# First loads of a layer kernel: block 0 of x and weight piece 0 in two 64-row halves on both queues, blocks 2 and 3 of x in one load

## The chip, the cores and the metric

One core of one Trainium2 chip runs the kernel. The metric is device microseconds of one execution, the median of several runs. PE (TensorE) does the matrix multiplications and transposes, DVE (VectorE) and ACT (ScalarE) the elementwise work, POOL (GpSimd) some DMA, and SP (SyncE) issues most loads. ACT issues a few loads too, from its own instruction stream: while it issues one it does nothing else.

## The reference

A pre-norm transformer layer in bf16, sequence length S = 2048, width D = 512:

```python
h  = x + A(layernorm(x))      # A: qkv = n @ wqkv; 32 heads of 16; each position attends to
                              # 8 positions pos, pos-2, ..., pos-14 (masked below 0); @ wo
h2 = h + B(layernorm(h))      # B: (relu(n @ W_gate) * (n @ W_up)) @ W_down, F = 1376
# layernorm(x) = (x - mean) / sqrt(var + 1e-5) over the 512 columns of a row
```

## The kernel before, in words

The 2048 rows of x are 16 blocks of 128 rows; a chunk is 4 blocks, and the kernel goes through 4 chunks, with the work of neighbouring chunks interleaved. A table of ranks (`RANK`) fixes the order of all steps on every engine; the change does not touch it. Ahead of the planned steps stands `setup()`, which issues the first loads and builds small constants.

**The first loads.** `x_sm` holds all of x; `x_sm[:, j, :]` is block j, 128 rows of 1 KB. `wqk_sb[:, j, :]` is weight piece j: rows 128j to 128j+127 of the q and k columns, 128 rows of 2 KB. SP issued, in this order: block 0, block 2, piece 2, block 4, block 5, piece 3; and behind them blocks 6 and 7 (L343), the v weights (L344), chunks 2 and 3 of x (L346), the output weights (L348). ACT issued block 1, block 3, piece 0, piece 1, and behind these four its activation table is loaded (L328). Loads of x are L325 and of pieces L327 in the profile.

**Semaphores of the loads.** The framework gives the loads of SP and ACT eight semaphores in turn. A ninth load waits until the first, whose semaphore it takes over, has landed, and so on. In the listings below these semaphores are `DMAHW0` to `DMAHW7`; an instruction that reads a loaded tile waits for the semaphore of its load.

**Layer norm of chunk 0.** For blocks 0, 2 and 3 DVE takes the statistics (L492) and aggregates them (L495); for block 1 ACT sums the row (L476) and its squares (L482). ACT makes the scale factor of each block out of these with a logarithm and an exponential (L505 or L508, then L512). DVE writes the normalized rows (L553, L551 for block 1; tile `row`). PE transposes them (L582, tile `bank`), ACT evicts the transposes of blocks 0 and 1 (L598) and DVE those of blocks 2 and 3 (L596) into a tile `quad`. DVE's order is: statistics 0, 2, 3, with the aggregations between, then rows 0, 1, 2, 3. ACT's order is: sum 1, logarithm 0, squares 1, exponential 0, logarithms 1 and 2, exponentials 1 and 2, logarithm and exponential 3, evictions of 0 and 1.

**Projection of chunk 0.** The first six q and k tiles (L623, weights `wqk_sb`) are summed over the four pieces in the order 0 (for columns 0 to 255, blocks 0 and 1), 0 (columns 256 to 511, blocks 2 and 3), 2, 1, 3. Before all this PE multiplies zeros (L437, `warm`). The rest of the kernel, attention, output projection and the gated MLP (L1010, L1064), is not touched.

The program's first lines that matter:

```python
x_rows = A_x.rearrange("b (tb p) d -> p (b tb) d", p=P)      # P = 128, BPC = 4 blocks a chunk
w3_r = A_wqkv.rearrange("(dt p) f -> p dt f", p=P)
WQ = ([("a", 0, 2 * P, 0), ("b", 2 * P, CS, 0), ("c", 0, CS, 2), ("d", 0, CS, 1), ("e", 0, CS, 3)],)
XS = ((0, 1),)                                               # chunk 0, block 1: sums on ACT
```

Of the kernel before, what the change touches and what calls it, by code (L numbers as in the profile page):

```python
# [8 lines left out]
P = 128  # L9
# [192 lines left out]
def kernel(  # L202
# [11 lines left out]
    nc = tc.nc  # L214
    Bsz, S, D = A_x.shape
# [23 lines left out]
    BPC = CS // P  # L239
# [4 lines left out]
    x_rows = A_x.rearrange("b (tb p) d -> p (b tb) d", p=P)  # L244
# [20 lines left out]
    x_sm = sb.tile([P, NTB, D], BF16, name="x_sm")  # L265
    wqk_sb = sb.tile([P, NT, 2 * D], BF16, name="wqk_sb")
# [39 lines left out]
    def f_load(n, i):  # L306
        if n == "d":
            lo, hi = (0, 5) if i == 0 else (5, NFF)
            nc.sync.dma_start(
                wd_sb[:, lo:hi, :], B_W_down[lo * P:hi * P, :].rearrange("(ft p) n -> p ft n", p=P))  # L310
            if FTAIL and i:
                nc.sync.dma_start(wd_sb[:FTAIL, NFF, :], B_W_down[NFF * P:F, :])
        elif n == "g":
            nc.sync.dma_start(wgu_sb[:, :, 0, :], B_W_gate.rearrange("(dt p) f -> p dt f", p=P))
        else:
            w = B_W_up.rearrange("(dt p) f -> p dt f", p=P)
            nc.sync.dma_start(wgu_sb[:, 2 * i:2 * i + 2, 1, :], w[:, 2 * i:2 * i + 2, :])

    def setup():

        w3_r = A_wqkv.rearrange("(dt p) f -> p dt f", p=P)
        for q, n, j in ((nc.sync, "x", 0), (nc.scalar, "x", 1), (nc.sync, "x", 2), (nc.scalar, "x", 3), (nc.sync, "w", 2),
                        (nc.scalar, "w", 0), (nc.sync, "x", BPC), (nc.scalar, "w", 1), (nc.sync, "x", BPC + 1), (nc.sync, "w", 3)):
            if n == "x":
                q.dma_start(x_sm[:, j:j + 1, :], x_rows[:, j:j + 1, :])  # L325
            else:
                q.dma_start(wqk_sb[:, j:j + 1, :], w3_r[:, j:j + 1, 0:2 * D])  # L327
        nc.scalar.preload_act_table_set("natural_log_exp_and_others")  # L328
        V.memset(warm[:], 0.0)
        make_identity(nc, identity[:])  # L330
        nc.gpsimd.memset(eps_t[:, 0:1], EPS)
        nc.gpsimd.memset(eps_t[:, 1:2], EPS * D * D)
        nc.gpsimd.iota(ci[:], pattern=[[0, 1]], base=0, channel_multiplier=1)
        nc.gpsimd.iota(sel_i[:], pattern=[[1, H]], base=0, channel_multiplier=0)
        nc.gpsimd.iota(sp_i[:], pattern=[[1, H], [0, DQ]], base=0, channel_multiplier=0)
        nc.gpsimd.iota(sm_i, pattern=[[0, 4], [1, H]], base=0, channel_multiplier=0)
        nc.gpsimd.iota(mk_i[:], pattern=[[1, PADL]], base=0, channel_multiplier=0)
        nc.gpsimd.memset(kT[:, :, 0:PADL], 0.0)
        nc.gpsimd.memset(vT[:, :, 0:PADL], 0.0)


        for j in range(BPC + 2, 2 * BPC):
            nc.sync.dma_start(x_sm[:, j:j + 1, :], x_rows[:, j:j + 1, :])  # L343
        nc.sync.dma_start(wv_sb[:], w3_r[:, :, 2 * D:3 * D])  # L344
        for tk in range(2, NCK):
            nc.sync.dma_start(x_sm[:, tk * BPC:(tk + 1) * BPC, :], x_rows[:, tk * BPC:(tk + 1) * BPC, :])  # L346

        nc.sync.dma_start(wo_sb[:], A_wo.rearrange("(p t) f -> p t f", t=NT))  # L348
        if "g" not in LATE:
            f_load("g", 0)  # L350

        for n, (op, by) in enumerate(((ALU.arith_shift_right, 2), (ALU.bitwise_and, H - 1),
                                      (ALU.arith_shift_right, 5))):
            V.tensor_scalar(out=tmp[:, n:n + 1], in0=ci[:], scalar1=by, scalar2=None, op0=op)
        V.tensor_copy(out=cf[:, 0:3], in_=tmp[:])
        V.tensor_scalar(out=cf[:, 2:3], in0=cf[:, 2:3], scalar1=1.0 * DIL, scalar2=None, op0=ALU.mult)
        V.tensor_scalar(out=cf[:, 3:4], in0=cf[:, 2:3], scalar1=4.0 * DIL, scalar2=None, op0=ALU.add)
        V.tensor_scalar(out=sel[:], in0=sel_i[:], scalar1=cf[:, 0:1], scalar2=None, op0=ALU.is_equal)
        V.tensor_scalar(out=spread[:], in0=sp_i[:], scalar1=cf[:, 1:2], scalar2=None, op0=ALU.is_equal)
        V.tensor_scalar(out=same[:], in0=sm_i, scalar1=cf[:, 1:2], scalar2=None, op0=ALU.is_equal)  # L360
        for hf in range(2):
            V.tensor_scalar(out=mask[:, hf, :], in0=mk_i[:], scalar1=cf[:, 2 + hf:3 + hf],
                            scalar2=None, op0=ALU.is_ge)
# [242 lines left out]
    for tk in range(NCK):  # L606
# [353 lines left out]
        for f0 in range(0, NFT, 2):  # L960
# [77 lines left out]
            n, fs = len(fts), P if fts[-1] < NFF else FTAIL  # L1038
# [66 lines left out]
    for o in plan.ops:  # L1105
        n = o.key[0] if o.key else ""
# [7 lines left out]
    with tc.manual_schedule():  # L1114
        setup()
        for op in todo:
            if op.fn is not None:
                op.fn()
# [35 lines left out]
```

## Time and profile before

| | |
|---|---|
| timed runs | 191.07, 191.41, 191.52 us (median 191.41) |
| the profiled execution | 190.84 us, of which the span from the first to the last instruction is 189.0 us |
| granted TensorE clock | 1.000 |
| PE busy | 183.6 us (97%) |
| DVE, ACT, POOL busy | 149.3, 116.9, 25.1 us |
| chain that ended last | PE 94%, ACT 3% |

Times in a row are microseconds from the span's start unless marked ns. A row of the timeline gives the start, the length, the engine (an added q means its sequencer, so the issue of a DMA), the line, what was written and read, and in brackets the idle time of the engine before it and what ended it. A row of the DMA issues gives how many of a kind were issued, KB each, and the time from issue to landing. Queue q1 holds the loads of SP, q10 those of ACT.

### The profile page before, as it was taken

What the parts mean: (1) busy time and instruction counts of PE and PEld (TensorE: products, weight loads), DVE (VectorE), ACT (ScalarE), POOL (GpSimd) and SP (SyncE); (2) the same over time, 40 slices, a digit from 0 to 9 for tenths busy, and PEclk for the clock granted to TensorE, in tenths of its full rate; (3) what the DMA queues carried; (4) which work ended last, traced back from release to release, by engine and by line L of the source; (5) the groups of instructions that cost most, each with busy time, mean ns of one, the idle gap of its engine ahead of it and who ended that gap; (6) DMA issues with size and microseconds to landing.
All of it is one profiled execution on the core that took longest, in us unless ns stands there. A gap on an engine that the chain in (4) does not pass through costs nothing.

```text
span 189.0 us, 2973 instructions
## 1 busy us (share of the span) xinstructions
PE 183.6 (97%) x1077; PEld 92.3 (49%) x1077; DVE 149.3 (79%) x226; ACT 116.9 (62%) x241; POOL 25.1 (13%) x46
## 2 busy tenths in 40 slices
PE   7798999999999999999999999999999999999994
PEld 7554455654454445544444464444445445454543
DVE  6999999999999999999999986999758401315233
ACT  4689999965676868923656686134874602675700
POOL 3000503300000032310051250025100000000000
DMA  5998488980987979993238998659923500102014
GB/s 156 330 343 351 92 200 141 194 166 0 184 229 185 292 153 182 183 214 63 59 68 153 173 179 238 114 111 180 214 49 88 107 4 0 55 3 56 0 62 132
DMA packets 27742, 26.96 MB, mean 143 GB/s; under 512 B 14704, under 2 KB 23248, under 8 KB 27728
## 3 DMA queue, kind: packets, MB, share of 16 engines
q1 hardware_dynamic: 23696, 15.47, 30.4%
q0 software_dynamic: 3312, 10.49, 29.3%
q10 hardware_dynamic: 720, 0.82, 1.3%
q8 instruction: 8, 0.13, 0.3%
q14 instruction: 6, 0.05, 0.1%
HBM read 8.42 MB, written 2.10 MB: 56 GB/s over the span
## 4 chain that ended last, share of the span: by engine, by line
PE 94%; ACT 3%; ACTq 1%; issue 0%; DVE 0%
PE bank L1010 37%; PE bank L623 22%; PE bank L1064 20%; PE bank L933 7%; PE bank L973 3%; PE bank L680 3%; PE bank L582 1%; PE bank L732 1%; ACT L328 1%; ACT quad L598 1%; ACTq L327 0%; ACTq L325 0%; PE bank L777 0%; ACT row L548 0%; ACT junk L482 0%; ACT rs L508 0%
## 5 line engine op out<-in xcount | busy, mean ns | idle before, releaser
L1010 PE MATMUL bank<-quad,wgu_sb 128*128 128x512 bf16 x320 | 72.4, 379 | 0.0
L1010 PEld LDWEIGHTS <-wgu_sb 128*128 128x128 bf16 x320 | 31.0, 98 | 37.1 <-issue 1.3
L1064 PE MATMUL bank<-wd_sb,gT 128*128 128x512 bf16 (+3 forms) x198 | 39.6, 355 | 0.0
L1020 ACT ACTIVATE gr<-bank 128x512 bf16<-128x512 f32 x40 | 23.1, 604 | 13.1 <-PE bank L1010 10.2
L623 PE MATMUL bank<-quad,wqk_sb 128*128 128x512 bf16 (+1 forms) x134 | 30.0, 370 | 0.0
L1064 PEld LDWEIGHTS <-gT 128*128 128x128 bf16 (+1 forms) x198 | 18.5, 98 | 19.9
L1017 ACT CAST up_sb<-bank 128x512 bf16<-128x512 f32 x30 | 16.9, 602 | 14.9 <-PE bank L1010 12.3
L674 DVE TENSOR_TENSOR big<-quad,kT 128x4096 bf16<-128x4096 bf16 x11 | 25.1, 2286 | 0.0
L852 DVE TENSOR_TENSOR big<-big,vT 128x4096 bf16<-128x4096 bf16 x11 | 24.7, 2289 | 0.0
L1041 DVE TENSOR_TENSOR gT<-gr,up_sb 128x1024 bf16<-128x1024 bf16 x20 | 13.6, 689 | 9.4 <-ACT gr L1020 6.3
L895 POOL DMA_DIRECT2D big<-big x14 | 12.4, 883 | 64.5 <-DVE big L852 55.0
L623 PEld LDWEIGHTS <-wqk_sb 128*128 128x128 bf16 x134 | 14.9, 113 | 12.2 <-issue 0.6
L1072 DVE SCALAR_TENSOR_TENSOR row<-bank,iv,x_sm 128x512 bf16<-128x512 f32 (+2 forms) x10 | 6.2, 642 | 18.4 <-PE bank L1064 18.2
L482 ACT ACTIVATE junk<-x_sm,sm 128x512 bf16<-128x512 bf16 x17 | 12.2, 720 | 9.6 <-DVE x_sm L944 9.5
L623 PE MATMUL bank<-quad,wv_sb 128*128 128x512 bf16 x64 | 16.2, 380 | 0.0
L933 PE MATMUL bank<-wo_sb,quad 128*128 128x512 bf16 x64 | 14.8, 379 | 0.0
L855 DVE TENSOR_TENSOR big<-big 128x1024 bf16<-128x1024 bf16 (+2 forms) x20 | 12.9, 662 | 1.8 <-DMA big<-big 1.7
L944 DVE SCALAR_TENSOR_TENSOR x_sm<-x_sm,bank 128x512 bf16<-128x512 bf16 x16 | 10.7, 679 | 2.7 <-PE bank L933 2.7
L631 ACT CAST kT<-bank 128x512 bf16<-128x512 f32 x16 | 9.2, 591 | 3.2 <-PE bank L623 3.2
L631 ACT CAST quad<-bank 128x512 bf16<-128x512 f32 x16 | 9.2, 586 | 3.2 <-PE bank L623 3.2
L623 PEld LDWEIGHTS <-wv_sb 128*128 128x128 bf16 x64 | 6.9, 114 | 7.1 <-issue 1.3
L820 POOL DMA_DIRECT2D big<-ex x12 | 6.8, 591 | 23.8 <-DVE st L492 18.3
(85 smaller groups left out, 178.5 us busy)
## 6 DMA issues: line engine op xcount, KB each, us to landing
big<-big POOLq DMA_DIRECT2D x14, 512.0 KB, 5.4
big<-ex SPq DMA_DIRECT2D x20, 128.0 KB, 3.7
big<-ex POOLq DMA_DIRECT2D x12, 128.0 KB, 4.0
wgu_sb<-in_B_W_gate_dram SPq DMA_DIRECT2D x1, 1376.0 KB, 9.6
wgu_sb<-in_B_W_up_dram SPq DMA_DIRECT2D x2, 688.0 KB, 5.1
wd_sb<-in_B_W_down_dram SPq DMA_DIRECT2D x2, 640.0 KB, 5.4
x_sm<-in_A_x_dram SPq DMA_DIRECT2D x2, 512.0 KB, 7.4
x_sm<-up_sb POOLq DMA_DIRECT2D x4, 256.0 KB, 3.4
```

Source lines behind the costliest of these rows:

```text
L623: nc.tensor.matmul(mm.t[:, lo:hi], lhsT=wv_sb[:, dt, t:D:NT] if c == 2 else wqk_sb[:, dt, c * D + t:(c + 1) * D:NT], rhs=xnT.t[:, dt, lo:h ...
L631: nc.scalar.copy(out=o, in_=mm.t[:])
L674: V.tensor_tensor(out=pb.t[:].rearrange("p (t w) s -> p t w s", t=2), in0=q4, in1=k4, op=ALU.mult)
L852: V.tensor_tensor(out=mt.t[:], in0=ab.t[:], in1=v8, op=ALU.mult)
L855: V.tensor_tensor(out=mt.t[:, 0:n, :], in0=mt.t[:, 0:n, :], in1=mt.t[:, n:2 * n, :], op=ALU.add)
L895: nc.gpsimd.dma_start(mt.t[:, 0:4, :], mt.t[:, 4:8, :], accum_op=ALU.add)
L933: nc.tensor.matmul(od.t[:], lhsT=OT.t[:, t, j * P:(j + 1) * P], rhs=wo_sb[:, t, :], start=(t == 0), stop=(t == NT - 1 and tk not in RPE))
L1010: nc.tensor.matmul(mm.t[:fs, lo:hi], lhsT=wgu_sb[:, dt, g, ft * P: ft * P + fs], rhs=hnT.t[:, dt, lo:hi], start=(dt == 0), stop=(dt == NT ...
L1017: nc.scalar.copy(out=ub.t[:fs, i, :], in_=um.t[:fs, :])
L1020: nc.scalar.activation(out=gr.t[:fs, i, :], in_=gm.t[:fs, :], func=ACT.Relu, scale=-1.0 if tk in HX else 1.0)
L1041: V.tensor_tensor(out=gt.t[:fs, 0:n, :], in0=gr.t[:fs, 0:n, :], in1=ub.t[:fs, 0:n, :], op=ALU.mult)
L1064: nc.tensor.matmul(od.t[:, c0:c1], lhsT=gts[ft].t[:fs, ft % 2, j * P:(j + 1) * P], rhs=wd_sb[:fs, ft, c0:c1], start=(ft == 0), stop=(ft == ...
```

## The change

Block 0 of x is fetched as rows 0 to 63 by SP and rows 64 to 127 by ACT; weight piece 0 likewise, as the third load of each queue. Block 1 goes to SP's second place; ACT's second load is now blocks 2 and 3 together, 128 rows of 2 x 1 KB. Piece 2 is SP's fourth load and piece 1 ACT's fourth. Behind them nothing changes in order. SP has one load more than before, ACT as many.

```diff
     def setup():
 
         w3_r = A_wqkv.rearrange("(dt p) f -> p dt f", p=P)
-        for q, n, j in ((nc.sync, "x", 0), (nc.scalar, "x", 1), (nc.sync, "x", 2), (nc.scalar, "x", 3), (nc.sync, "w", 2),
-                        (nc.scalar, "w", 0), (nc.sync, "x", BPC), (nc.scalar, "w", 1), (nc.sync, "x", BPC + 1), (nc.sync, "w", 3)):
+        hp = P // 2
+        hp = P // 2
+        for q, n, j in ((nc.sync, "x", 0), (nc.scalar, "x", 0), (nc.sync, "x1", 1), (nc.scalar, "xx", 2), (nc.sync, "w", 0),
+                        (nc.scalar, "w", 0), (nc.sync, "w1", 2), (nc.scalar, "w1", 1), (nc.sync, "x1", BPC), (nc.sync, "x1", BPC + 1), (nc.sync, "w1", 3)):
+            lo, hi = (0, hp) if q is nc.sync else (hp, P)
             if n == "x":
+                q.dma_start(x_sm[lo:hi, j:j + 1, :], x_rows[lo:hi, j:j + 1, :])
+            elif n == "xx":
+                q.dma_start(x_sm[:, j:j + 2, :], x_rows[:, j:j + 2, :])
+            elif n == "x1":
                 q.dma_start(x_sm[:, j:j + 1, :], x_rows[:, j:j + 1, :])
+            elif n == "w":
+                q.dma_start(wqk_sb[lo:hi, j:j + 1, :], w3_r[lo:hi, j:j + 1, 0:2 * D])
             else:
                 q.dma_start(wqk_sb[:, j:j + 1, :], w3_r[:, j:j + 1, 0:2 * D])
```

On SP, the start of its program before (loads of x and of weight pieces, with the semaphores that their issue waits for; the first three wait for none):

```order
L325 DMA x_sm<-in_A_x_dram 128x512 x2
L327 DMA wqk_sb<-in_A_wqkv_dram 128x1024
L325 DMA x_sm<-in_A_x_dram 128x512
L325 DMA x_sm<-in_A_x_dram 128x512 [waits DMAHW0_49]
L327 DMA wqk_sb<-in_A_wqkv_dram 128x1024 [waits DMAHW1_49]
L343 DMA x_sm<-in_A_x_dram 128x512 [waits DMAHW2_49]
```

and now:

```order
L328 DMA x_sm<-in_A_x_dram 64x512
L332 DMA x_sm<-in_A_x_dram 128x512
L334 DMA wqk_sb<-in_A_wqkv_dram 64x1024
L336 DMA wqk_sb<-in_A_wqkv_dram 128x1024
L332 DMA x_sm<-in_A_x_dram 128x512 [waits DMAHW0_49]
L332 DMA x_sm<-in_A_x_dram 128x512 [waits DMAHW1_49]
L336 DMA wqk_sb<-in_A_wqkv_dram 128x1024 [waits DMAHW2_49]
L352 DMA x_sm<-in_A_x_dram 128x512 [waits DMAHW3_49]
```

Piece 3 (the last 128x1024) waited for the second semaphore, block 0's; it now waits for the third, that of the double block. Block 4 waited for no load and now waits for a half of block 0.

On ACT, the start of its program before, down to the sum of block 1 and the first logarithm:

```order
L325 DMA x_sm<-in_A_x_dram 128x512 x2
L327 DMA wqk_sb<-in_A_wqkv_dram 128x1024 x2
L328 ACT_TABLE_LOAD
L476 ACTIVATE junk,sm_121<-x_sm 128x512 [waits DMAHW0_49]
L508 ACTIVATE rs_131<-mv_117,eps_t 128x1 [waits DVE_49,Pool_49]
```

and now:

```order
L328 DMA x_sm<-in_A_x_dram 64x512
L330 DMA x_sm<-in_A_x_dram 128x2x512
L334 DMA wqk_sb<-in_A_wqkv_dram 64x1024
L336 DMA wqk_sb<-in_A_wqkv_dram 128x1024
L337 ACT_TABLE_LOAD
L485 ACTIVATE junk,sm_121<-x_sm 128x512 [waits DMAHW3_49]
L517 ACTIVATE rs_131<-mv_117,eps_t 128x1 [waits DVE_49,Pool_49]
```

Four loads stand ahead of the table load as before; the sum of block 1 now waits for a load of SP, not for ACT's own first one.

On DVE, the statistics of blocks 0, 2 and 3 of chunk 0 and the first normalized row, before:

```order
L492 BN_STATS st_113<-x_sm 128x6 [waits DMAHW1_49]
L495 BN_AGGR mv_117<-st_113 128x2 [waits DVE_49]
L492 BN_STATS st_114<-x_sm 128x6 [waits DMAHW3_49]
L495 BN_AGGR mv_117<-st_114 128x2 [waits DVE_49]
L492 BN_STATS st_115<-x_sm 128x6 [waits DMAHW2_49]
L553 TENSOR_SCALAR row_104<-x_sm,mv_117,rs_131 128x512 [waits Activation_49]
```

and now:

```order
L501 BN_STATS st_113<-x_sm 128x6 [waits DMAHW1_49,DMAHW0_49]
L504 BN_AGGR mv_117<-st_113 128x2 [waits DVE_49]
L501 BN_STATS st_114<-x_sm 128x6 [waits DMAHW2_49]
L504 BN_AGGR mv_117<-st_114 128x2 [waits DVE_49]
L501 BN_STATS st_115<-x_sm 128x6
L562 TENSOR_SCALAR row_104<-x_sm,mv_117,rs_131 128x512 [waits Activation_49]
```

The order of the work is the same; block 0's statistics wait for two halves, block 2's for the double block, and block 3's for no load of their own.

## The prediction

> **What bounds the kernel now.** I read the page first, then the waits of PE over the whole span, then the chain that ended last and the engines one by one over the first 8 us, and last the DMA queues in short windows. The page's first row and PE's waits:
>
> ```profile
> PE 183.6 (97%) x1077; PEld 92.3 (49%) x1077; DVE 149.3 (79%) x226; ACT 116.9 (62%) x241; POOL 25.1 (13%) x46
> ...
> PE bank L437 <- DVE warm L329: 1.0, 1, 1.0
> PE bank L582 <- DVE row L553: 1.0, 1, 1.0
> PE bank L582 <- ACT row L548: 0.5, 1, 0.5
> ```
>
> PE is busy for 183.6 of 189.0 us, and its only listed waits are three, all before 18 us. So after the start there is next to nothing in which a late start could be made up: what the first projection matmul (L623) loses or gains, the end loses or gains. The change touches only the first loads; the question is what they do to that matmul. The chain of waits at the start, times in us from the span's start, then length:
>
> ```profile
> 2.63 1.28 ACT L328
> ...
> 3.93 0.33 ACT junk L476
> ...
> 6.73 0.97 ACT quad L598 x2
> ...
> 7.74 1.28 PE bank L623 x8
> ```
>
> ACT issues its four loads, loads its table until 3.91, sums block 1 (L476) at 3.93 and goes on without a real break to the transposes' evictions (L598), which release L623 at 7.74. No load stands in this chain. DVE is as tight beside it:
>
> ```profile
> 3.30 0.69 DVE L492 BATCH_NORM_STATS2 st<-x_sm 128x6 f32<-128x512 bf16 x1
> 4.03 0.18 DVE L495 BATCH_NORM_AGGREGATE mv<-st 128x2 f32<-128x6 f32 x1
> 4.13 0.66 DVE L492 BATCH_NORM_STATS2 st<-x_sm 128x6 f32<-128x512 bf16 x1
> 4.83 0.18 DVE L495 BATCH_NORM_AGGREGATE mv<-st 128x2 f32<-128x6 f32 x1
> 4.95 0.70 DVE L492 BATCH_NORM_STATS2 st<-x_sm 128x6 f32<-128x512 bf16 x1
> 5.67 0.41 DVE L553 TENSOR_SCALAR row<-x_sm,mv,rs 128x512 bf16<-128x512 bf16 x1
> ...
> 5.45 0.18 ACT L512 ACTIVATE rs<-rs 128x1 f32<-128x1 f32 x1
> ```
>
> The statistics of blocks 0, 2 and 3 (3.30, 4.13, 4.95) run one behind the other up to the first normalized row at 5.67, and ACT's factor for that row (L512) is done at 5.63: two chains that meet within 0.04 us. From 5.67 to 7.74 there are 2.07 us of transposes and evictions that the change leaves alone.
>
> **The change part by part.** What the loads did before (landing counted from the issue). The first pair was issued at 0.74 on both queues, the second, as half of each "x2" row, at about 1.17 (ACT) and 1.20 (SP):
>
> ```profile
> x_sm<-in_A_x_dram ACTq DMA_DIRECT2D x1, 128.0 KB, 2.7
> x_sm<-in_A_x_dram SPq DMA_DIRECT2D x1, 128.0 KB, 2.5
> ...
> x_sm<-in_A_x_dram ACTq DMA_DIRECT2D x1, 128.0 KB, 3.8
> x_sm<-in_A_x_dram SPq DMA_DIRECT2D x1, 128.0 KB, 2.7
> ...
> 0.73 0.90 ACTq L325 DMA_DIRECT2D x_sm<-in_A_x_dram  x2
> 1.67 0.94 ACTq L327 DMA_DIRECT2D wqk_sb<-in_A_wqkv_dram  x2
> ...
> 0.74 0.87 SPq L325 DMA_DIRECT2D x_sm<-in_A_x_dram  x2
> 1.66 0.42 SPq L327 DMA_DIRECT2D wqk_sb<-in_A_wqkv_dram  x1
> ```
>
> So block 0 landed at 3.3, block 1 at 3.4 to 3.5, block 2 at 1.20 + 2.7 = 3.9 and block 3 at 1.17 + 3.8 = 4.97 by the rounded row (its reader started at 4.95). Block 2 had 0.2 us to spare against 4.13, block 3 none, and it needed none.
>
> *Block 0 in halves.* It may land sooner than 3.3; its reader is the first L492. But DVE's next step waits for block 2, and ACT's chain starts from the table load. Price: zero either way, up to a landing 0.2 us later.
>
> *ACT's issues.* Four before, four after. Four took 2.63 - 0.73 = 1.90 us, up to the table load. A half may take less: the shortest issue in the trace is 0.33 us (the row of 4.95 below), against 0.45 for each of ACT's two (0.90 x2), so two halves save at most 0.24. The double block may take more: the nearest row is a load of 4 blocks, 1.07 for two, so 0.54 and at most 0.09 more. The table load moves by -0.24 to +0.09 and the factor of L512 is ready at 5.39 to 5.72. I take 0, and DVE covers all of it, as follows.
>
> ```profile
> 4.95 0.33 SPq L343 DMA_DIRECT2D x_sm<-in_A_x_dram  x1
> 7.35 1.07 SPq L346 DMA_DIRECT2D x_sm<-in_A_x_dram  x2
> ```
>
> *Blocks 2 and 3 in one load.* This is the term that counts. One semaphore now stands for both, so the statistics of block 2 wait until block 3 is in as well. No row shows a load of this kind at this place. It cannot be before block 2's own 3.9, where it costs nothing. The nearest row above is block 3's 4.95, the same last byte of the same 512 KB of x. The queue counts tell which is nearer (packets, MB, share of 16 engines; q10 is ACT's queue, q1 SP's; first 3.4 to 3.8 us, then 4.6 to 5.0):
>
> ```profile
> q1 hardware_dynamic: 23, 0.03, 79.8%
> q10 hardware_dynamic: 68, 0.06, 44.3%
> ...
> q1 hardware_dynamic: 35, 0.07, 45.9%
> q10 hardware_dynamic: 35, 0.07, 45.2%
> ...
> q1 hardware_dynamic: 302, 0.29, 29.6%
> q10 hardware_dynamic: 284, 0.27, 22.6%
> ```
>
> The last two rows are 0 to 3.8 us. Two blocks are 256 rows of 1 KB and, if every engine closes each load with one small packet, 32 more: 288. ACT's queue had started 284 packets by 3.8, so all but a few of block 3 were through by then and a late rest made it 4.95. With a landing some 0.5 after the last packet (an estimate: block 2 landed at 3.9, when SP's queue had long turned to weights), an undisturbed pair would land near 4.3; with a late rest at 4.95. I take 4.4, in the middle of 3.9 and 4.95. Then L492 of block 2 starts at 4.42 instead of 4.13, +0.29, everything behind it on DVE is back to back, the first row starts at 5.96 instead of 5.67 (ACT's factor at 5.72 at the latest is hidden), and L623 starts at 8.03: **+0.3**. Bounds of the term: 0 and 4.97 - 4.13 = 0.84; more is rival B.
>
> *Weight piece 0 in halves.* The pieces on ACT's queue were issued at 1.67 and about 2.15 (the two take 0.94), the first piece on SP's (piece 2) at 1.66, and they landed after:
>
> ```profile
> wqk_sb<-in_A_wqkv_dram SPq DMA_DIRECT2D x1, 256.0 KB, 5.0
> wqk_sb<-in_A_wqkv_dram ACTq DMA_DIRECT2D x1, 256.0 KB, 5.2
> ...
> wqk_sb<-in_A_wqkv_dram ACTq DMA_DIRECT2D x1, 256.0 KB, 5.7
> ```
>
> Piece 0 landed at 6.9 and is first used at 7.74: 0.8 us to spare. The halves stand at the same depth in the queues; sooner brings nothing, and even at the 7.85 of the last ACT piece they would be in time for 8.03. Price zero.
>
> *SP's queue waits.* SP has one load more, so each later load waits for a different earlier one: block 4, which waited for none, now for a half of block 0, and piece 3 for the double block (issue at 3.87 before, about 4.4 now). Piece 3 has no spare time, as the weight loads of PE show:
>
> ```profile
> 3.87 0.44 SPq L327 DMA_DIRECT2D wqk_sb<-in_A_wqkv_dram  x1
> ...
> wqk_sb<-in_A_wqkv_dram SPq DMA_DIRECT2D x1, 256.0 KB, 5.1
> x_sm<-in_A_x_dram SPq DMA_DIRECT2D x1, 128.0 KB, 4.3
> ...
> 8.97 0.44 PEld L623 LDWEIGHTS <-wqk_sb 128*128 128x128 bf16 x3 [0.20 <-DMA wqk_sb<-in_A_wqkv_dram]
> ```
>
> It was issued at 3.87 and landed 5.1 later, at 8.97, and PE's loader took it at that moment. The load behind it was issued 1.07 us later (4.95) and landed only 0.3 later (9.25): the queue ahead sets these landings, not the issue, and the bytes ahead are the same. So I take zero. If the issue did set it, piece 3 would land at 4.42 + 5.1 = 9.5, against a need that has moved to 8.97 + 0.3 = 9.27: 0.25 more at worst. Block 4 feeds statistics of the next chunk, which no PE wait names. The loads behind (v weights, rest of x, wo, gate) may move by half a microsecond; the three waits of PE above name none of them.
>
> **Sum.** 190.84 (the profiled execution: 189.0 of span and 1.84 around it) + 0.3 = 191.1. The timed runs have their median at 191.41, 0.57 above that execution; the same +0.3 on it gives **191.7**. The forecast's own range is 191.4 to 191.98: a shift that a measurement can hardly tell from none (0.3% is 0.57 us, about what one can tell here).
>
> **Rivals.**
>
> *B, the double block shares turns with the weights: slower.* SP's queue holds half of block 0 and block 1, 192 rows, before its weight half; ACT's holds 64 + 256 = 320 rows before its own. If the engines take from the two queues in equal turns, as the 35 and 35 packets of 4.6 to 5.0 show, 128 rows of x are left on ACT's queue when SP's turns to weights. Each then lets a weight row pass, 0.459 x 6.4 / 35 = 0.084 us of one engine, and the first ones 0.798 x 6.4 / 23 = 0.22 (6.4 is 16 engines for 0.4 us). 128 x 0.084 / 16 = 0.67, plus 23 x 0.14 / 16 = 0.2 for the slow first rows: the pair lands at 4.4 + 0.87 = 5.3, L623 shifts by 1.2, and the time is 191.41 + 1.2 = **192.6** (192.0 to 193.0). It decides from a landing at 4.7 on, where the shift passes 0.57. Against it stands that ACT's queue passed 68 packets from 3.4 to 3.8 while SP's, already at weights, passed 23: block 3 went ahead of them. Also, the Trainium skill ("DMA: Bandwidth & Descriptors", the section on queues, rings and completion order) says that an engine drains a whole packet, typically 9 to 17 descriptors, from one queue before it turns to the other; by that rule the double block, some 16 rows per engine, would go ahead whole and B would fall away, which leaves the +0.3. The equal 35 and 35 neither bear this out nor refute it. Chance 0.36.
>
> *C, the halves bring a gain.* The timed runs lie 0.2 to 0.7 above the profiled one. If that is block 0 or 1 coming late in them, an earlier block 0 and a shorter ACT issue take it away: about 191.41 - 0.57 = **190.8**. For it: the two chains before 5.67 leave 0.04 us of slack. Against it: block 1, which ACT needs first, moves from first to second place, and block 2 must come by 4.13. The Trainium skill ("DMA: Bandwidth & Descriptors", the rules for kernel authors) advises against splitting a load into two partition halves, since both go over the same 16 engines; by it block 0 would land no sooner than 3.3 and C would have nothing. In this trace two loads of 128 KB issued together landed 0.2 apart, at 2.5 and 2.7, which fits. Chance 0.07.
>
> *D, nothing moves.* The double block lands by 4.13, ACT's chain stays the last: **191.4**. For it: block 2's 3.9. Against it: the last x bytes had not all started by 3.8. Chance 0.07.
>
> **How the numbers follow.** The forecast has 0.50, B 0.36, C 0.07, D 0.07. Faster by over 0.3% (below 190.84) is C, 0.07. Slower by over 0.3% (above 191.98) is B, 0.36. Within is the forecast and D: 0.57. The range 191.2 to 192.7 holds the forecast, D and some two thirds of B, and leaves out C and B's upper end, about 2 in 10.
>
> **What would show it.** Right: in the changed profile the second L492-type statistic (now L501) starts at 4.2 to 4.6, waiting for a load, the first row about 1.5 us later, and the first projection matmul at 7.9 to 8.3; the table load and ACT's sum of block 1 stand within 0.2 us of their old places; PE's wait before the transposes grows from 1.0 to about 1.3. B: that statistic starts after 4.7, with weight packets on SP's queue before the double block is in. C or D: the first projection matmul at 7.74 or before. Wrong altogether: a new PE wait for weights behind 8 us, or a shift at the start that is not found again at the end.

## The result and the profile after

| | before | after |
|---|---|---|
| timed runs, median (range), us | 191.41 (191.07 to 191.59) | 194.01 (192.24 to 195.33) |
| ratio to before, 95% interval | | 1.0113 (1.0064 to 1.0161) |
| profiled execution; its span, us | 190.84; 189.0 | 192.24; 190.5 |
| granted TensorE clock of the profiled execution | 1.000 | 0.999 |
| first projection matmul starts, us | 7.74 | 8.73 |

The change makes the kernel slower, by 1.1%; the forecast of 191.7 and its range up to 192.7 were too low. Disturbed runs (here the one of 195.33, later the one of 198.08 and the three of 196.1 to 196.85 without warm-up) are left out of all ratios and means.

The profiled execution of after is its fastest run. In it the loss lies at the start and stays: the first projection matmul comes 0.99 later and the last store is issued 1.00 later; the rest of the span's growth of 1.5 comes after that store. The last store, before and after:

```profile
186.66 0.35 ACTq L1078 DMA_DIRECT2D out_dram<-row  x1
...
187.66 0.35 ACTq L1087 DMA_DIRECT2D out_dram<-row  x1
```

The page's first row, as shown of before:

```profile
PE 183.4 (96%) x1059; PEld 93.0 (49%) x1077; DVE 149.4 (78%) x226; ACT 116.8 (61%) x241; POOL 25.1 (13%) x46
```

and PE's waits:

```profile
PE bank L591 <- DVE row L562: 1.1, 1, 1.1
PE bank L446 <- DVE warm L338: 1.0, 1, 1.0
PE bank L591 <- ACT row L557: 0.5, 1, 0.5
```

PE's work is the same (18 matmuls fewer are recorded, but as many weight loads), and its wait before the transposes has grown by only 0.1: the same 77 warm-up matmuls ended at 6.06 in this execution and at 5.16 in that of before, so part of the delay doesn't show as a wait. The chain of waits at the start names what is new (start, length, in us):

```profile
0.74 0.61 SPq L328
...
1.41 3.48 DMA x_sm<-in_A_x_dram
...
4.92 0.02 ACT junk L485
...
7.72 0.97 ACT quad L607 x2
...
8.73 0.74 PE bank L632 x5
```

Before, this chain began with ACT's issues and its table load, and no load stood in it. Now a load does: SP's second one, block 1, issued at 1.41 and landed 3.48 later, at 4.89. ACT's sum of block 1 (L485, L476 before) starts at 4.92 instead of 3.93. The two issuing engines and ACT's first work, from the timeline:

```profile
0.74 0.56 ACTq L328 DMA_DIRECT2D x_sm<-in_A_x_dram  x1
1.34 0.60 ACTq L330 DMA_DIRECT2D x_sm<-in_A_x_dram  x1
1.97 0.50 ACTq L334 DMA_DIRECT2D wqk_sb<-in_A_wqkv_dram  x1
2.50 0.60 ACTq L336 DMA_DIRECT2D wqk_sb<-in_A_wqkv_dram  x1
3.13 1.28 ACT L337 ACT_TABLE_LOAD   x1 [3.13 <-issue]
4.92 0.63 ACT L485 ACTIVATE junk<-x_sm 128x512 bf16<-128x512 bf16 x1 [0.50 <-DMA x_sm<-in_A_x_dram]
...
0.74 0.61 SPq L328 DMA_DIRECT2D x_sm<-in_A_x_dram  x1
1.41 0.81 SPq L332 DMA_DIRECT2D x_sm<-in_A_x_dram  x1
```

Every issue in these rows is longer than before. The halves take 0.56 and 0.61, though they move half the bytes of a block that took 0.45 on ACT; the load behind a half takes 0.60 on ACT and 0.81 on SP. So the table load starts at 3.13 instead of 2.63 (+0.50), ends at 4.41, and ACT then still waits 0.50 for block 1: together the 0.99. The landing alone sets this start: with the table load at its old place ACT would have waited until 4.92 just the same. DVE and PE follow:

```profile
4.38 0.69 DVE L501 BATCH_NORM_STATS2 st<-x_sm 128x6 f32<-128x512 bf16 x1 [0.16 <-DMA x_sm<-in_A_x_dram]
...
6.66 0.41 DVE L562 TENSOR_SCALAR row<-x_sm,mv,rs 128x512 bf16<-128x512 bf16 x1 [0.78 <-ACT rs L521]
7.12 1.55 PE L591 MATMUL bank<-identity,row 128*128 128x128 bf16 x16 [1.06 <-DVE row L562]
8.73 6.68 PE L632 MATMUL bank<-quad,wqk_sb 128*128 128x256 bf16 x35
```

The double block let the statistics of block 2 start at 4.38, 0.25 later than before. That delay is then covered: DVE waits 0.78 for ACT's factor before it writes the first row at 6.66. ACT's chain is the late one.

The profile explains 1.0 to 1.4 us; the ratio stands for 2.2. The granted clock of the timed runs shows where the rest may be. The run of 192.24 has 0.999, those of 193.51, 194.01 and 194.52 have 0.991. 0.9% of 192 us is 1.7 us, what one stretch of 3.4 us at half clock would take away; profiles further down show such stretches.

### The profile page after: what moved, and what is told of

Same layout as the page of the kernel before. It is cut to its first block, busy times and chain, and to the rows that moved or that the text cites. A ratio compares the mean times of both kernels' runs of the same rounds, so it can differ in the third digit from the quotient of the medians.

```text
span 190.5 us, 2958 instructions
## 1 busy us (share of the span) xinstructions
PE 183.4 (96%) x1059; PEld 93.0 (49%) x1077; DVE 149.4 (78%) x226; ACT 116.8 (61%) x241; POOL 25.1 (13%) x46
## 4 chain that ended last, share of the span: by engine, by line
PE 92%; ACT 2%; DMA 2%; issue 1%; SPq 0%; DVE 0%
PE bank L1019 36%; PE bank L632 21%; PE bank L1073 20%; PE bank L942 7%; PE bank L982 3%; PE bank L689 3%; DMA x_sm<-in_A_x_dram 2%; PE bank L591 1%; PE bank L741 1%; PE bank L786 1%; ACT quad L607 1%; ACT row L557 0%; ACT junk L491 0%; SPq L328 0%; ACT rs L517 0%
## 5 line engine op out<-in xcount | busy, mean ns | idle before, releaser
L632 PE MATMUL bank<-quad,wv_sb 128*128 128x512 bf16 x61 | 15.7, 380 | 0.3 <-issue 0.2
```

Of the source, the lines that this page charges most:

```text
L632: nc.tensor.matmul(mm.t[:, lo:hi], lhsT=wv_sb[:, dt, t:D:NT] if c == 2 else wqk_sb[:, dt, c * D + t:(c + 1) * D:NT], rhs=xnT.t[:, dt, lo:h ...
```

## The experiments

Theory 1, formed from the profile after: block 1 sits in SP's second place behind ACT's double block, which is issued 0.07 earlier and goes first. Theory 2: the cut into 64 rows itself is slow to issue and delays the load behind it. The rival for the runs at clock 0.991: they are an accident of the chip, not of PE's wait. Each time stands against the runs of before on the same chip (medians 191.58, 191.61 and 191.45 in the three groups). Of long lines the diffs show only the items that change.

**Block 1 on ACT, the double block on SP.** Everything else as after.

```diff
-                        (nc.sync, "x1", 1), (nc.scalar, "xx", 2),
+                        (nc.sync, "xx", 2), (nc.scalar, "x1", 1),
```

> The changed kernel with the second loads of the two queues exchanged: block 1 on ACT, the double block on SP. Theory 1 (rows are handed to the engines load by load in the order of issue, so in the changed kernel block 1 stood behind all of the double block, which ACT had issued 0.07 us earlier, and landed at 4.89): block 1 now lands by 4.0 and ACT's sum of block 1 waits only for the table load, at about 4.4 instead of 4.92; the first projection matmul at 8.2 to 8.4 instead of 8.73. Rival (block 1 is late because SP's queue is served worse, or because halves slow all loads): block 1 lands no sooner than 4.6 on ACT as well, and the first projection matmul stays at 8.6 or later.

Measured: 192.84 (191.88 to 194.19), ratio 1.0071 (1.0042 to 1.01). The timeline of this kernel:

```profile
1.41 0.79 SPq L329 DMA_DIRECT2D x_sm<-in_A_x_dram  x1
...
3.11 1.28 ACT L336 ACT_TABLE_LOAD   x1 [3.11 <-issue]
...
4.41 0.63 ACT L484 ACTIVATE junk<-x_sm 128x512 bf16<-128x512 bf16 x1
5.46 0.69 DVE L500 BATCH_NORM_STATS2 st<-x_sm 128x6 f32<-128x512 bf16 x1 [1.25 <-DMA x_sm<-in_A_x_dram]
```

Block 1 is now in time (ACT starts at 4.41, as its table load ends), but the double block on SP lands 4.03 after its issue instead of 3.0 on ACT, and DVE waits 1.25 for it; the first projection matmul starts at 8.92, not at the 8.2 to 8.4 that theory 1 expected. SP's second load is late whichever it is. Six runs at clock 0.999 or more average 192.45, four at 0.991 average 193.75: 1.3 us lie between.

**Only block 0 in row halves.** No double block, piece 0 whole; SP issues its half, block 1, block 3, piece 2, ACT its half, block 2, pieces 0 and 1.

```diff
-  (nc.sync, "x1", 1), (nc.scalar, "xx", 2), (nc.sync, "w", 0), (nc.scalar, "w", 0),
+  (nc.sync, "x1", 1), (nc.scalar, "x1", 2), (nc.sync, "x1", 3), (nc.scalar, "w1", 0),
```

> Block 0 in halves, but no double block and piece 0 whole: SP issues half 0, block 1, block 3, piece 2; ACT half 0, block 2, piece 0, piece 1. Theory 2 (a half load takes longer to issue, 0.56 to 0.61 us against 0.40, and with it ACT's table load moves from 2.63 to 3.13): the two first issues take 0.55 or more, the table load starts at 2.8 or later, and the first projection matmul comes 0.2 to 0.5 later than in the kernel before (7.9 to 8.3). Rival (the issues were slowed by the double block, not by the halves): first issues of 0.40 to 0.45, the table load at 2.6 to 2.7, the first projection matmul at 7.6 to 7.9.

Measured: 193.98 (191.86 to 194.72), ratio 1.0107 (1.0062 to 1.0152). The DMA issues (the second loads, then the halves; KB, and us from issue to landing):

```profile
x_sm<-in_A_x_dram ACTq DMA_DIRECT2D x1, 128.0 KB, 2.4
x_sm<-in_A_x_dram SPq DMA_DIRECT2D x1, 128.0 KB, 4.0
x_sm<-in_A_x_dram SPq DMA_DIRECT2D x1, 64.0 KB, 2.5
x_sm<-in_A_x_dram ACTq DMA_DIRECT2D x1, 64.0 KB, 2.1
```

and ACT's first sum in the timeline:

```profile
5.45 0.63 ACT L484 ACTIVATE junk<-x_sm 128x512 bf16<-128x512 bf16 x1 [1.23 <-DMA x_sm<-in_A_x_dram]
```

ACT's second load has 128 rows now, no double block is there, and block 1 on SP still takes 4.0 to land, at 5.43. Theory 1 falls. One 64-row cut alone brings the whole loss. Theory 2 had the issues right (0.56 and 0.61, the table load at 2.94), but it priced them alone: the first projection matmul starts at 9.27 instead of 7.9 to 8.3, because of the late landing.

**More and less warm-up.** NWARM's second number counts the later group of warm-up matmuls of zeros on PE, which end shortly before the transposes. After with 28 instead of 15:

```diff
-    NWARM, NFILL = (62, 15), (0, 0, 0)
+    NWARM, NFILL = (62, 28), (0, 0, 0)
```

> The changed kernel with 28 instead of 15 wide warm-up matmuls on zeros, which fill most of PE's longer wait before the transposes (1.06 us in its profile). Theory 3 (the four timed runs above the profiled one, at clocks of 0.991, lost TensorE's full clock for a few us because PE waits longer at the start): nearly all runs at clock 0.999 to 1.0 and a median of 192.3 to 192.9. Rival (their spread is that of the first loads, the clock only goes along): median 193.5 to 194.5 as without.

Measured: 193.2 (192.55 to 193.93), ratio 1.0088 (1.0061 to 1.0114). None of its six runs is at 0.991 (0.997 to 1.0). The first projection matmul starts at 9.06, block 1 landed at 5.22: the loads are as late as ever, and only the clock is kept. The median lies between what the theory expected (up to 192.9) and what its rival did (193.5 and more): the clock is right, the gain smaller than thought.

Before with none (0 instead of 15), so that PE's wait grows with no load moved:

```diff
-    NWARM, NFILL = (62, 15), (0, 0, 0)
+    NWARM, NFILL = (62, 0), (0, 0, 0)
```

> The kernel before with none instead of 15 wide warm-up matmuls, so that PE waits 0.8 us longer before the transposes while the loads and everything else stay. Theory 3: runs at a clock of about 0.991 appear, and the median rises by 0.8 to 1.8 us (192.2 to 193.2) with no load moved. Rival (spread of the loads): the clock stays at 1.0 and the median within 0.4 of 191.41.

Measured: 194.0 (192.55 to 196.85), ratio 1.008 (1.0047 to 1.0113); the four runs behind the ratio are 192.55 to 194.0, all at clock 0.991, with a median of 192.8 as expected. PE's longest wait in this kernel:

```profile
PE bank L582 <- DVE row L553: 1.6, 1, 1.6
```

and three stretches of it (from:to, length, busy time and instructions of PE, PEld, DVE, ACT and POOL, granted clock, DMA share, GB/s):

```profile
4.60:8.00 3.40, 1.68 (x19) 1.25 (x20) 3.19 (x10) 3.08 (x13) 0.00 (x0) 1.00 0.92 319
8.00:11.40 3.40, 3.18 (x12) 1.46 (x11) 2.94 (x8) 0.59 (x1) 0.00 (x0) 0.50 0.88 281
11.40:15.00 3.60, 3.60 (x21) 2.15 (x20) 2.72 (x5) 2.82 (x7) 0.00 (x0) 1.00 1.05 365
```

and the middle stretch of the kernel before:

```profile
8.00:11.40 3.40, 3.40 (x22) 2.14 (x20) 3.40 (x9) 1.66 (x3) 0.00 (x0) 1.00 0.92 274
```

The first projection matmul starts at 7.76, as before, yet the stretch from 8.0 to 11.4 runs at half clock and holds 12 matmuls instead of 22. A wait of 1.6 ahead of it is enough, and nothing of the change is in this kernel: PE's idle time loses the clock.

**Only piece 0 in row halves.** x is loaded as before.

```diff
-  (nc.sync, "x", 0), (nc.scalar, "x", 0), (nc.sync, "x1", 1), (nc.scalar, "xx", 2),
+  (nc.sync, "x1", 0), (nc.scalar, "x1", 1), (nc.sync, "x1", 2), (nc.scalar, "x1", 3),
```

> Only weight piece 0 in two 64-row halves; blocks 0 to 3 of x as in the kernel before. Theory (a 64-row load and the load behind it take 0.1 to 0.4 us longer to issue; what stands behind them on ACT, the table load, comes later): ACT's third and fourth issue take 0.5 and 0.6 instead of 0.45 each, the table load starts at 2.75 to 2.9 instead of 2.63, the first projection matmul at 7.85 to 8.1, the time 0.1 to 0.5 above before (0.0 to 0.3%). Rival (the weight halves cost nothing, all the loss is in the halves of block 0): table load at 2.6 to 2.7 and a time within 0.2 of before.

Measured: 191.69 (191.47 to 192.31), ratio 1.0002 (0.9988 to 1.0016). The issues, first of SP, then of ACT:

```profile
0.74 0.89 SPq L331 DMA_DIRECT2D x_sm<-in_A_x_dram  x2
1.67 0.59 SPq L333 DMA_DIRECT2D wqk_sb<-in_A_wqkv_dram  x1
2.31 0.81 SPq L335 DMA_DIRECT2D wqk_sb<-in_A_wqkv_dram  x1
...
0.74 0.92 ACTq L331 DMA_DIRECT2D x_sm<-in_A_x_dram  x2
1.69 0.54 ACTq L333 DMA_DIRECT2D wqk_sb<-in_A_wqkv_dram  x1
2.26 0.59 ACTq L335 DMA_DIRECT2D wqk_sb<-in_A_wqkv_dram  x1
```

The 64-row loads take 0.59 and 0.54 here too, and the loads behind them 0.81 and 0.59. The table load starts at 2.88 and the first projection matmul at 7.99, 0.25 later each, as the theory expected, and PE waits 0.3 for weights in the profiled execution. The median is 0.08 above before's: the interval allows the 0.25 and allows none.

**Only the double block.** Blocks 2 and 3 in one load on SP's second place; nothing is cut. ACT issues block 1 and pieces 0 and 1.

```diff
-  (nc.sync, "x", 0), (nc.scalar, "x", 0), (nc.sync, "x1", 1), (nc.scalar, "xx", 2), (nc.sync, "w", 0), (nc.scalar, "w", 0),
+  (nc.sync, "x1", 0), (nc.scalar, "x1", 1), (nc.sync, "xx", 2), (nc.scalar, "w1", 0),
```

> Only blocks 2 and 3 in one load, as SP's second; blocks 0 and 1 and piece 0 whole; ACT has three loads ahead of its table. The term of the prediction: the pair lands at 4.2 to 4.9, the statistics of block 2 start then, the first projection matmul at 7.8 to 8.5, the time 0.1 to 0.8 above before. Rival (the double block was never the cost): the pair lands by 4.2, the table load at about 2.2 gives ACT time in hand, the first projection matmul at 7.3 to 7.75, the time at or below before.

Measured: 191.9 (191.47 to 193.07), ratio 1.0014 (0.9996 to 1.0033). In the profiled execution the double block landed 4.16 after its issue, at 5.36, later than the 4.2 to 4.9 expected; the rows of piece 0 from ACT's second place ran beside its own. DVE waited 1.06 for it, and that run has a clock of 0.991 and took 193.07, the longest. Ten of the twelve runs are at 0.998 or more, with 191.47 to 192.23. The interval doesn't exclude no change.

**After with column halves.** The same loads at the same places, but each half has all 128 rows and half the columns.

```diff
-            lo, hi = (0, hp) if q is nc.sync else (hp, P)
+            h = 0 if q is nc.sync else 1
...
-                q.dma_start(x_sm[lo:hi, j:j + 1, :], x_rows[lo:hi, j:j + 1, :])
+                q.dma_start(x_sm[:, j:j + 1, h * D // 2:(h + 1) * D // 2], x_rows[:, j:j + 1, h * D // 2:(h + 1) * D // 2])
...
-                q.dma_start(wqk_sb[lo:hi, j:j + 1, :], w3_r[lo:hi, j:j + 1, 0:2 * D])
+                q.dma_start(wqk_sb[:, j:j + 1, h * D:(h + 1) * D], w3_r[:, j:j + 1, h * D:(h + 1) * D])
```

> The changed kernel with its halves cut by columns: 128 rows of 256 (piece 0: 512) columns on each queue, all else the same. Theory (it is the 64 rows that make the issue and the rows behind it late): the first issues take 0.40 to 0.47, the table load starts at 2.6 to 2.8, block 1 lands by 4.2, the first projection matmul at 7.8 to 8.3, the median 0.0 to 0.7 above before. Rival (two halves of any form are slow, or the double block is): first issues 0.55 or more or block 1 after 4.6, the first projection matmul at 8.6 or later, the median 1.0 or more above before.

Measured: 191.37 (191.27 to 191.73), ratio 0.9985 (0.997 to 1.0); all twelve runs at clock 0.997 or more. The timeline:

```profile
0.74 0.39 SPq L328 DMA_DIRECT2D x_sm<-in_A_x_dram  x1
1.19 0.42 SPq L332 DMA_DIRECT2D x_sm<-in_A_x_dram  x1
...
2.67 1.28 ACT L337 ACT_TABLE_LOAD   x1 [2.67 <-issue]
...
3.96 0.63 ACT L485 ACTIVATE junk<-x_sm 128x512 bf16<-128x512 bf16 x1
4.30 0.69 DVE L501 BATCH_NORM_STATS2 st<-x_sm 128x6 f32<-128x512 bf16 x1 [0.26 <-DMA x_sm<-in_A_x_dram]
```

The half's issue is 0.39 instead of 0.61, the one behind it 0.42 instead of 0.81, the table load stands at 2.67 instead of 3.13, and block 1 landed at 3.53 instead of 4.89. The first projection matmul starts at 7.78. With the same bytes at the same places on the same queues, all of the loss goes when the cut runs through the columns. So the cut into 64 rows is the cause; theory 2 holds in that, with the landing behind the half as the larger part.

**Before with more warm-up** (22 instead of 15), to see whether before loses clock as well.

```diff
-    NWARM, NFILL = (62, 15), (0, 0, 0)
+    NWARM, NFILL = (62, 22), (0, 0, 0)
```

> The kernel before with 22 instead of 15 wide warm-up matmuls: PE's wait before the transposes falls from 1.0 to about 0.6, nothing else moves. Theory 3 (the clock is lost in an execution when PE waits too long at the start): the runs of before that lie above 192 go, the median falls by 0 to 0.4. Rival (the spread of before comes from the loads alone): median within 0.2 of before and the same spread.

Measured: 191.51 (191.19 to 192.54), ratio 0.9999 (0.9982 to 1.0016), clocks 0.998 to 1.0. The rival holds: two runs are still above 192. Nothing was to be had, since before keeps its clock in all but one of the 35 runs of this group (192.75, at 0.991).

**All of the first four blocks in row halves.** Blocks 0 and 1 each in two 64-row halves, then blocks 2 and 3 together in two; the weights whole.

```diff
-  (nc.sync, "x1", 1), (nc.scalar, "xx", 2), (nc.sync, "w", 0), (nc.scalar, "w", 0),
-  (nc.sync, "w1", 2), (nc.scalar, "w1", 1), (nc.sync, "x1", BPC),
+  (nc.sync, "x", 1), (nc.scalar, "x", 1), (nc.sync, "xh", 2), (nc.scalar, "xh", 2),
+  (nc.sync, "w1", 2), (nc.scalar, "w1", 0), (nc.sync, "x1", BPC), (nc.scalar, "w1", 1),
...
+            elif n == "xh":
+                q.dma_start(x_sm[lo:hi, j:j + 2, :], x_rows[lo:hi, j:j + 2, :])
```

> All four blocks of chunk 0 in 64-row halves on both queues (blocks 2 and 3 as one pair of halves), weight pieces whole. So far the load behind a half was the slow one as well: 0.59 us on ACT and 0.80 on SP to issue, its rows on SP 1.0 to 1.4 us late. Theory A (a 64-row load is slow by itself): every half takes 0.55 us or more to issue, the table load starts at 3.0 or later, the first projection matmul at 8.3 or later. Theory B (it is the step from 64 rows to 128 rows on one queue that costs): the second and third halves take 0.40 to 0.47, the first whole load behind them 0.6 or more, and block 1 lands by 4.2.

Measured: 194.14 (193.09 to 194.57), ratio 1.0127 (1.01 to 1.0154). Issues and table load:

```profile
0.74 1.21 ACTq L327 DMA_DIRECT2D x_sm<-in_A_x_dram  x2
1.98 0.65 ACTq L329 DMA_DIRECT2D x_sm<-in_A_x_dram  x1
...
0.74 1.48 SPq L327 DMA_DIRECT2D x_sm<-in_A_x_dram  x2
...
3.79 1.28 ACT L338 ACT_TABLE_LOAD   x1 [3.79 <-DMA x_sm<-in_A_x_dram]
```

Three 64-row loads in a row take 1.21 + 0.65 on ACT; the slowness is the half's own and comes again with each, not only at a change of form. That is theory A. The table load is 1.16 later than before, with five loads ahead of it on ACT instead of four. Block 1, in halves, landed at 3.57 and 3.88, as theory B had it: SP's second load, now itself a half, took 2.5 to land. But the last half of blocks 2 and 3 landed at 5.65, and the first projection matmul starts at 9.21.

**Column halves of block 0 alone, without the double block.** The same as the second experiment, except for the cut.

```diff
-            lo, hi = (0, hp) if q is nc.sync else (hp, P)
+            h = 0 if q is nc.sync else 1
...
-                q.dma_start(x_sm[lo:hi, j:j + 1, :], x_rows[lo:hi, j:j + 1, :])
+                q.dma_start(x_sm[:, j:j + 1, h * D // 2:(h + 1) * D // 2], x_rows[:, j:j + 1, h * D // 2:(h + 1) * D // 2])
```

> Block 0 in column halves of 128 rows, block 1 on SP, block 2 on ACT, block 3 on SP, weight pieces whole: as in the run with row halves of block 0 alone, but cut by columns. If only the form of the halves made that run slow: first issues 0.40 to 0.45, all x landed by 4.3, the first projection matmul at 7.6 to 7.8 and a median at or up to 0.4 below before. If splitting block 0 is itself a cost: a first matmul after 8.0 and a median 0.4 or more above before.

Measured: 191.56 (191.24 to 193.21), ratio 1.0003 (0.9984 to 1.0021). Against 193.98 for the row cut, with the cut as the one difference in the code. The DMA issues in the same order as there:

```profile
x_sm<-in_A_x_dram ACTq DMA_DIRECT2D x1, 128.0 KB, 2.8
x_sm<-in_A_x_dram SPq DMA_DIRECT2D x1, 128.0 KB, 2.5
x_sm<-in_A_x_dram ACTq DMA_DIRECT2D x1, 64.0 KB, 2.3
x_sm<-in_A_x_dram SPq DMA_DIRECT2D x1, 64.0 KB, 2.2
```

SP's second load lands 2.5 after its issue, not 4.0; the halves themselves take about as long as the row halves (2.2 and 2.3 against 2.1 and 2.5). The form of the half hurts the load behind it on SP, not the half. SP's third load, block 3, landed at 5.04 instead of the 4.3 expected, and the first projection matmul starts at 7.87.

**After once more, and after with 36 warm-up matmuls.** Run side by side, the first unchanged, for the share of runs that lose clock and its price.

```diff
-    NWARM, NFILL = (62, 15), (0, 0, 0)
+    NWARM, NFILL = (62, 36), (0, 0, 0)
```

> The changed kernel once more, for its executions beside those of the next run on the same chip. Theory 3 (in most executions TensorE also loses its full clock for one stretch of 3.4 us): most runs at 0.991, these 1 to 1.7 us above the runs at 0.999 to 1.0, median 193.2 to 194.3. Rival (the first loads alone spread): the runs at 0.991 and those at 1.0 have the same times within 0.4.

> The changed kernel with 36 instead of 15 wide warm-up matmuls, so that PE works almost until the transposes. Theory 3: no run at 0.991, median 192.3 to 193.1, 0.6 to 1.5 below the changed kernel in the same call; what is left above before, 0.8 to 1.5, is the late block 1. Rival: median as the changed kernel's within 0.4.

Measured: after again 193.93 (192.51 to 198.08), ratio 1.0095 (1.0062 to 1.0129); with 36 warm-ups 193.03 (192.6 to 193.67), ratio 1.0078 (1.0054 to 1.0102), all clocks 0.998 to 1.0. The profiled execution of after again is the one of 198.08. It shows at its start what happens to the clock in after itself: PE's wait before the transposes, the stretch around it and the next one.

```profile
PE bank L591 <- DVE row L562: 2.1, 1, 2.1
...
4.24:7.65 3.41, 1.33 (x24) 1.12 (x22) 2.16 (x7) 2.56 (x12) 0.00 (x0) 1.00 0.98 292
7.65:11.06 3.41, 3.16 (x23) 2.47 (x22) 2.93 (x8) 1.47 (x4) 0.00 (x0) 0.50 0.77 243
```

The wait is 2.1 here and was 1.1 in the first profile of after. The warm-up matmuls ended earlier (5.39 instead of 6.06) and block 1 landed later (5.24 instead of 4.89). Why this execution is the longest of all isn't shown in full; a second stretch at half clock, from 38.4 us, is part of it.

Over both groups of after, seven runs at 0.991 average 194.00 and three at 0.999 or 1.0 average 192.52: 1.5 us apart. What is left with the clock kept is 1.1 us in those three (192.52 against 191.41 to 191.45), but 1.6 with more warm-up (193.2 and 193.03, each against before in its own group). The three may be those in which the loads came earliest: in the profiles with 28 and 36 warm-ups block 1 landed at 5.22 and 5.27 and the first projection matmul started 1.3 to 1.4 later than before, against 4.89 and 1.0 in the run of 192.24. So the loads' part is 1.1 to 1.6 us and the clock's, in seven runs of ten, 1.0 to 1.5.

## Why the prediction was wrong

**What bounds the kernel: right.** The delay of the first projection matmul is found again at the end, 0.99 and 1.00. That ACT's chain and DVE's meet within 0.04, so that each has no slack, was right as well; it is what made ACT's wait for block 1 count in full.

**The double block: right, and covered.** It landed at 4.36 against the 4.4 taken, the statistics of block 2 stood at 4.38 against 4.42. That it hit so closely is partly luck: in three other profiles of the same loads (28 and 36 warm-ups, after again) it landed at 4.54 to 5.10. This was the one term of the sum, and the one that the time doesn't contain: DVE has 0.78 to spare in after, and 0.42 or more in the other three.

**"ACT's issues ... The table load moves by -0.24 to +0.09 ... I take 0": wrong, but not what sets the time.** It moved by +0.50. The half of block 0 alone moves it by 0.31, that of piece 0 alone by 0.25. A half was priced by the shortest issue in the trace, 0.33, that of a 128-row load, on the guess that fewer bytes issue faster. Before has no load of 64 rows, so the bound came from another form. Column halves, with the same bytes and 128 rows, take 0.39 to 0.41 in place of 0.56 to 0.61: it is the cut, not the bytes. In after this delay is hidden, since block 1 lands still later.

**"Block 0 in halves ... Price: zero either way": wrong, and this is the step that failed.** The halves themselves landed at 2.88 and 3.21, before the old 3.3. What was not priced is the load behind them. SP's second place went to block 1, on which ACT waits; the prediction mentions that move only against rival C and gives it no term. The place alone would have cost nothing: with column halves block 1 landed there at 3.53, against 3.48 on ACT before. Behind a row half it landed at 4.89, which puts ACT's sum of block 1 and the first projection matmul 0.99 later; in other profiles with this cut SP's whole second load landed at 5.2 to 5.4.

**No term for the clock: the second step that failed, and about half of the loss where it strikes.** The prediction saw that PE's wait before the transposes would grow, to about 1.3, and priced the wait alone. Seven of ten executions of after lost clock; they lie 2.6 us above before (194.00 against 191.41), and 1.0 to 1.5 of that are the clock. The stretch at half clock is seen in five profiles: after again, less warm-up, block 0 in row halves, the double block alone with its wait of 1.9, all row halves. The runs of after with more warm-up have none of it. What decides when the warm-up ends, and with it which executions lose the clock, isn't shown.

**Piece 0 in halves: about zero, but not for the reason given.** The weights come in time, as predicted. But the issues are long here too: alone they move the table load and the first projection matmul by 0.25, which the ratio of 1.0002 (0.9988 to 1.0016) can't tell from none. In after this too is hidden behind block 1.

**SP's queue waits: about right.** Piece 3 was issued at 4.39 (4.4 expected), landed at 9.96, and PE's loader waited 0.26 for it (0.20 before), but beside a shift of 1.0 it didn't add to the end.

**The rivals.** B gave 192.6 (192.0 to 193.0) and the sign, but too little and by another way: the double block did not share turns with weights in after. Its mechanism can be seen where double block and weight stand at the same depth (the double block alone), and its price there was 0.0014 (-0.0004 to 0.0033) of the time. C's rule from the Trainium skill ("DMA: Bandwidth & Descriptors", the rules for kernel authors: two transfers to disjoint partition halves, "Don't bother") points the right way, but expects no gain, where the runs show a loss of 1.07% with that cut of block 0 alone. C and D are out.

**What stays open.** Why a load of 64 rows takes longer to issue than one of 128, and why the whole block behind it on SP takes 1.1 to 1.5 longer from issue to landing than with column halves, while on ACT the second load takes 2.4 to 3.8 with row halves, against 2.8 to 3.1. The delay on SP is there from the first row on: with only block 0 cut, SP's queue had started no packet by 2.35 us with the row cut and 129 with the column cut. No run separates how the loads are put together from how the queues pass them.

## What to carry to other kernels

Price a load of a new shape by a row of that shape or not at all, and price the load behind it on the same queue as well; if no row has the shape, the bound is open upward and the range must say so. To split a load over two queues, cut along the columns and keep all 128 rows: this costs nothing here (0.9985, 0.997 to 1.0), though it gains too little to be told from none. A wait of TensorE ahead of a dense stretch of matmuls is priced twice, once as the wait and once as the clock that may go with it, and the clock of each run tells which it was.

## What the runs showed of the hardware

- **A load of 64 rows is issued slower than one of 128.** Of x 0.56 to 0.62 us in first place, against 0.39 to 0.41 with 128 rows, whole or half; of a weight piece 0.49 to 0.59, against 0.42 to 0.49. The load right behind a half of block 0 takes 0.59 to 0.61 on ACT and 0.79 to 0.81 on SP, against 0.42 to 0.49 without the row cut.
- **On SP a whole block behind it lands late.** From issue to landing 3.5 to 4.0 us for block 1, against 2.3 and 2.5 with column halves in the same order of loads, and 2.5 for a half behind a half.
- **A short gap in TensorE's work halves the clock.** In the five profiles that lost it, TensorE waited 1.6 to 2.1 us between its warm-up and the transposes, and the clock was then 0.50 for 3.4 us; with waits of up to 1.2 it stayed at 1.00. The Trainium skill ("TensorE: Matmul & The Clock Gate", the section on why this matters for your kernels) asks for no idle gaps above about 3 us between matmul bursts. Taken as the wait alone, less than that was enough here. But from the end of the warm-up to the first projection matmul, with the transposes counted into the gap, it is 3.2 to 3.9 us where the clock fell and at most 2.8 where it stayed, which agrees with the Trainium skill. No run here separates the two ways of counting.
- **An earlier landing can be worth nothing.** With column halves, block 0 landed at 2.91 and 3.07 instead of about 3.3 in the version without the double block, and its time was 1.0003 of before (0.9984 to 1.0021): ACT's chain starts from the table load, which stood at 2.65 as before (2.63).
